# Pooled v of the first batch summed on TensorE out of loaded v tiles, and the first FFN conversion queued behind the 13th attention unit

## The chip, the cores and the metric

The kernel runs on one core of one Trainium2 chip. The metric is the device time of one execution in microseconds (us), and the time of a kernel is the median of its runs. Of the engines, PE is TensorE (PEld its weight loads), DVE is VectorE, ACT is ScalarE, POOL is GpSimd, and SP only issues DMA transfers. Each engine takes its instructions strictly in the order in which they stand in its queue.

## What is computed

Attention runs over 2 batches, 8 heads, 576 positions and 64 values per head, in two forms whose outputs are added. Then comes a softplus FFN (1152 tokens, 512 to 2048 to 512), and then eight gated experts. Cut to what matters here:

```python
q_d = q.reshape(B, H, Sd, factor, D).mean(axis=3)      # factor 4, Sd = 144
k_d = k.reshape(B, H, Sd, factor, D).mean(axis=3)
v_d = v.reshape(B, H, Sd, factor, D).mean(axis=3)
out_up = np.repeat(sm_attn(q_d, k_d, v_d), factor, axis=2)
mask = np.abs(pos[:, None] - pos[None, :]) < factor
...
attn_out = out_up + out_local                          # local: softmax inside the mask
h = x @ w_in                                           # x: attn_out as 1152 x 512
x = (np.maximum(h, 0.0) + np.log1p(np.exp(-np.abs(h)))) @ w_out
...
out += P[:, e:e + 1] * (np.maximum(x @ w1[e], 0.0) @ w2[e])   # eight experts
```

## The kernel before

**Attention** is a list of units, each with four steps. A `pooled` unit (batch, half of the 144 pooled queries, pair of heads) makes scores `pd` from pooled q and k, exponentials `e`, transposes `ptd`, and the product `pvd` with the pooled v, `vd`. A `local` unit (batch, tile of 116 queries, half of the heads) makes masked scores `pl`, exponentials, transposes `ptl`, the product `pvl` with the loaded v tile `vw` (122 positions by 8 heads by 64 values and a one), and the transposed sum `xf`, which POOL splits into a high and a low part of `x`, the input of the FFN (a CAST and a subtraction). `emit` runs the units staggered, two units apart from step to step. There are 8 pooled and 10 local units in each batch, and unit number 9, 13 and so on below is the place in this mixed list, counted from 0. `warm` adds matmuls of zeros, `pz`, which keep TensorE busy while the first loads are under way.

**Pooling.** `pool_qk` sums q over groups of four positions on DVE (`qd`) and k on POOL (`ks`, `kd`), and ACT scales k. `load_vd` loads v a second time in another layout (`vr`, 640 KB for each half of the positions), and adds the four positions in two steps, `vs` and `vd`: on DVE for the first batch, on POOL for the second. Four `vr` tiles pass through two buffers of the pool `raw`, which the FFN weights use after them.

**FFN weights** arrive as doubles in tiles `raw` (1 MB each). `prep(n)` turns one tile into a high and a low part `w`: ACT makes `cs`, `cm` and the high part, DVE six operations in between (`cm` twice, `ch`, `ca`, `ch`, `cs`), POOL (DVE later) the low part. Products `ph` of the first FFN layer need `w` and `x`; `py` is the second layer.

**Order.** The table `at` says ahead of which unit an extra step is written: the loads of batch 1 at unit 1, `load_vd(1)` and the first two `raw` at 9, `pool_qk(1, p)` at 11 to 14, `prep(0)` to `prep(3)` at 16, 19, 23 and 29, the first FFN products from 22 on. A scheduler then sets the order on each engine within the bounds of the data and of `issue_after`, which keeps what is written inside it behind a named instruction. `local` step 3 loads the `vw` tile that is needed three tiles later, since there are three buffers.

Of the kernel before, what the change touches and what calls it, by code (L numbers as in the profile page):

```python
# [21 lines left out]
P = 128  # L22
# [54 lines left out]
class Net:  # L77
# [128 lines left out]
    def attention_pools(self, stack):  # L206
        tc = self.tc
        self.convp = stack.enter_context(tc.tile_pool(name="conv", bufs=1, side="right"))
        self.qkp = stack.enter_context(tc.tile_pool(name="qkp", bufs=NPAIR, side="right"))
        self.vwp = stack.enter_context(tc.tile_pool(name="vwp", bufs=3, side="right"))  # L210
# [35 lines left out]
    def pool_qk(self, b, p):  # L246

        nc = self.nc
        qd = self.atp.tile([P, 2, G], F32, tag="qd", name=f"qd{b}{p}", bufs=NPAIR)
        nc.vector.tensor_reduce(  # L250
            out=qd, in_=self.qT[b, p].rearrange("p h (g f) -> p h g f", f=POOLF), op=ALU.add, axis=AX.X
        )
        s = self.atp.tile([P, G, 2], F32, tag="ks", name=f"ks{b}{p}", bufs=2)
        k = self.kT[b, p]
        v = k.rearrange("p (g f) -> p g f", f=POOLF)
        nc.gpsimd.tensor_tensor(s, v[:, :, 0:2], v[:, :, 2:4], ALU.add)
        kd = self.atp.tile([P, G], F32, tag="kd", name=f"kd{b}{p}", bufs=NPAIR)
        nc.gpsimd.tensor_tensor(kd, s[:, :, 0], s[:, :, 1], ALU.add)
# [9 lines left out]
    def load_vd(self, b):  # L268
        nc = self.nc
        vd = self.atp.tile([GH, 2, H, DA], F32, tag="vd", name=f"vd{b}", bufs=2)  # L270
        nc.gpsimd.memset(vd[:, :, :, D:DA], 1.0)
        for hf in range(2):
            r = self.rawp.tile([GP, POOLF, DM], F32, tag="raw", name=f"vr{b}{hf}")
            nc.sync.dma_start(out=r, in_=self.a["vp"][b, hf].rearrange("p (f d) -> p f d", f=POOLF))
            s = self.convp.tile([GH, 2, DM], F32, tag=("ch", "cs")[hf], name=f"vs{b}{hf}", bufs=1)
            e = nc.vector if b == 0 else nc.gpsimd
            e.tensor_tensor(s, r[:GH, 0:2], r[:GH, 2:4], ALU.add)
            sv = s.rearrange("p f (h d) -> p f h d", h=H)
            e.tensor_tensor(vd[:, hf, :, 0:D], sv[:, 0], sv[:, 1], ALU.add)
        self.vd[b] = vd  # L280
        self.upT[b] = self.atp.tile([P, NPAIR, G], F32, tag="upT", name=f"upT{b}", bufs=2)

    def softmax_exp(self, ps, n, m, k, tag):

        nc = self.nc
        nm = self.atp.tile([m, n], F32, tag="nm" + tag, name="nm")
        nc.vector.tensor_reduce(out=nm, in_=ps, op=ALU.max, axis=AX.X, negate=True)
        e = self.atp.tile([m, n, k], F32, tag="e" + tag, name="e", bufs=3 if tag == "l" else 2)
        for j in range(n):
            nc.scalar.activation(e[:, j], ps[:, j], AF.Exp, bias=nm[:, j : j + 1])  # L290
        return e

    def pooled(self, b, hf, p):
# [25 lines left out]
            st["pt"] = pt  # L319

        def s3():
            ps = self.psa.tile([P, 512], F32, tag="a", name="pvd")[:GH, : 2 * DA].rearrange("p (j d) -> p j d", j=2)
            for j in range(2):
                for kh in range(2):
# [22 lines left out]
    def local(self, b, t, g):  # L347
# [33 lines left out]
        def s3():  # L381
            ps = self.psa.tile([P, 512], F32, tag="a", name="pvl")[:nq, : 4 * DA].rearrange("p (j d) -> p j d", j=4)
            for j in range(4):
                nc.tensor.matmul(  # L384
                    ps[:, j], lhsT=st["pt"][:, j], rhs=self.vw[b, t][:KW, 4 * g + j], start=True, stop=True
                )
            if g == 1 and NQT * b + t + 3 < B * NQT:
                self.load_vw(*divmod(NQT * b + t + 3, NQT))
# [326 lines left out]
    def run(self):  # L715
# [18 lines left out]
            self.pool_qk(0, p)  # L734
        self.constants()
        self.load_vd(0)
        for t in range(3):
            self.load_vw(0, t)

        def emit(items, rest):  # L740
# [25 lines left out]
                self.load_qk(1, p)  # L766

        def load_rest():
            self.load_vd(1)
            self.load_raw(1)  # L770

        def prep(n, lag):
# [4 lines left out]
                self.prep(n)  # L777


        at = {1: [load_second], 9: [load_rest]}  # L780
        for p in range(NPAIR):
            at.setdefault(11 + p, []).append(lambda p=p: self.pool_qk(1, p))
        for n, lag, u in zip(range(2 * NFT), (1, 1, 0, 0), (16, 19, 23, 29)):
            at.setdefault(u, []).append(lambda n=n, lag=lag: prep(n, lag))
        one, two, after = self.l1(0, 0, 1), self.l2(0, 0, 1), self.l1(0, 1, 1)
        for m, u in zip(one + two[:2], (22, 24, 26, 28, 30, 32)):
# [154 lines left out]
def arrange(i):  # L941
# [17 lines left out]
    m = [np.where(np.abs(r + o - c) < POOLF, f(0), f(-1e9)) for o in OFF]  # L959
    m = np.concatenate([np.stack(m, 1), np.zeros((P - QT, len(OFF), KW), f)], 0)  # L960
    out["mask"] = np.ascontiguousarray(m.astype(f))
    out["wg"] = np.ascontiguousarray(i["moe2_w_gate"].reshape(KD, P, E).transpose(1, 0, 2))

    def up(w):
# [36 lines left out]
```

## Time and profile before

| what | value |
|---|---|
| median of 3 runs (lowest to highest) | 1067.16 us (1064.26 to 1067.43) |
| the profiled execution | 1065.39 us, of which its span 1063.6 us |
| PE busy, share of the span | 1042.9 us, 98% |
| DVE, ACT, POOL busy | 74%, 41%, 16% |
| mean granted TensorE clock | 0.997 |

The span runs from the first instruction to the last, and 1.8 us of the execution lie outside it. A busy share is an average over the whole span. The attention, where the change is made, takes the first tenth of it; after that PE is busy all the time.

### The profile page before, as it was taken

The page shows a single profiled execution, that of the slowest core. Times are in us where ns is not written, and L with a number is a line of the kernel's source. Part 1 is how long each engine was busy: PE and PEld are TensorE (multiplying, and loading weights), DVE is VectorE, ACT ScalarE, POOL GpSimd, SP SyncE. Part 2 cuts the span into 40 slices and gives each one's busy share as a digit, 9 for nine tenths or more (in the row PEclk, how much of TensorE's full clock was granted, in tenths as well). Part 3 has the DMA queues.
Part 4 walks back from the last instruction along what each step waited for, and adds up shares of the span by engine and source line. Part 5 has one row for each costly group of instructions (what it writes and reads, how often), then busy time and mean ns, then how long its engine had stood idle before and what let it go on. Part 6 is the DMA issues. An engine that isn't in the chain of part 4 may idle for free.

```text
span 1063.6 us, 16117 instructions
## 1 busy us (share of the span) xinstructions
PE 1042.9 (98%) x6421; PEld 959.9 (90%) x6421; DVE 783.1 (74%) x1466; ACT 435.4 (41%) x815; POOL 165.8 (16%) x218
## 2 busy tenths in 40 slices
PE   7899999999999999999999999999999999999998
PEld 4789999999998899898989989898998989899896
DVE  6698699999997687784947658484765848576572
ACT  4688687766743433241413324141331414133130
POOL 3463300001112220211202011120201112020000
PEclk9899999999999999999999999999999999999999
DMA  9541032222111221111211111121111112110003
GB/s 250 163 153 62 2 120 79 79 80 80 41 40 40 79 80 40 40 41 39 80 40 40 41 40 41 40 80 40 40 40 40 41 40 79 40 41 1 1 2 89
DMA packets 13035, 63.99 MB, mean 60 GB/s; under 512 B 1760, under 2 KB 2016, under 8 KB 6496
## 3 DMA queue, kind: packets, MB, share of 16 engines
q1 hardware_dynamic: 12320, 61.79, 17.8%
q10 hardware_dynamic: 640, 1.18, 0.4%
q8 instruction: 50, 0.82, 0.3%
q14 instruction: 25, 0.20, 0.1%
HBM read 60.60 MB, written 2.36 MB: 59 GB/s over the span
## 4 chain that ended last, share of the span: by engine, by line
PE 87%; DVE 8%; ACT 2%; DMA 2%; POOL 1%; issue 1%; SPq 0%; DVEq 0%; ACTq 0%
PE po L586 37%; PE pu L537 33%; PE ph L444 7%; PE py L486 6%; PE pl L364 1%; DVE h L465 1%; DMA vr<-in_vp 1%; PE pvl L384 1%; DMA k<-in_k 1%; DVE r L461 1%; DVE l L462 1%; PE pvd L325 1%; DVE l L463 1%; DVE yp L498 0%; PE ptl L376 0%
## 5 line engine op out<-in xcount | busy, mean ns | idle before, releaser
L537 PE MATMUL pu<-T,a 128*128 128x320 f32 (+1 forms) x2688 | 354.2, 293 | 1.4 <-DVE yp L498 1.4
L537 PEld LDWEIGHTS pu<-T,a 128*128 128x128 f32 x2688 | 351.4, 188 | 3.0 <-issue 1.6
L608 DVE SCALAR_TENSOR_TENSOR acc<-po,prob,acc 128x512 f32<-128x512 f32 x126 | 94.1, 749 | 173.5 <-PE po L586 173.5
L586 PE MATMUL po<-w,h 128*128 128x512 f32 x960 | 221.3, 390 | 0.0
L586 PEld LDWEIGHTS po<-w,h 128*128 128x128 f32 x960 | 179.9, 188 | 37.3
L188 ACT CAST w<-raw 128x1024 fp32r<-128x1024 f32 x32 | 33.4, 1052 | 271.4 <-PE po L586 271.4
L586 PE MATMUL po<-w,h0a 128*128 128x512 f32 x576 | 142.3, 390 | 0.6 <-DVE w L189 0.6
L157 POOL TENSOR_TENSOR s<-raw 128x256 f32<-128x256 f32 x32 | 28.5, 891 | 677.6 <-DVE a L168 473.0
L586 PEld LDWEIGHTS po<-w,h0a 128*128 128x128 f32 x576 | 107.3, 188 | 22.5 <-DVE w L189 1.0
L486 PE MATMUL py<-h,w 128*128 128x384 f32 x576 | 104.0, 336 | 1.3 <-DVE h L465 0.8
L444 PE MATMUL ph<-x,w 128*128 128x384 f32 x576 | 104.1, 336 | 0.0
L486 PEld LDWEIGHTS py<-h,w 128*128 128x128 f32 x576 | 99.7, 188 | 2.3 <-DVE h L465 1.3
L444 PEld LDWEIGHTS ph<-x,w 128*128 128x128 f32 x576 | 99.8, 188 | 0.0
L549 ACT ACTIVATE h<-c 128x320 fp32r<-128x320 f32 x128 | 58.6, 468 | 79.8 <-DVE c L560 79.8
L550 DVE SCALAR_TENSOR_TENSOR h<-c,h 128x320 fp32r<-128x320 f32 x128 | 68.1, 540 | 0.3
L560 DVE TENSOR_TENSOR c<-v,pu 128x256 f32<-128x256 f32 (+1 forms) x128 | 57.8, 451 | 11.1 <-PE pu L537 8.2
L549 ACT ACTIVATE h0a<-c 128x256 fp32r<-128x256 f32 x96 | 37.5, 417 | 50.7 <-DVE c L560 50.4
L189 DVE TENSOR_TENSOR w<-raw,w 128x1024 fp32r<-128x1024 f32 x32 | 39.0, 1220 | 22.1 <-ACT w L188 22.1
L586 PE MATMUL po<-w,h0b 128*128 128x512 f32 x192 | 54.2, 389 | 0.0
L586 PEld LDWEIGHTS po<-w,h0b 128*128 128x128 f32 x192 | 36.0, 188 | 7.5
L558 ACT COPY p<-pu 128x256 f32<-128x256 f32 (+1 forms) x64 | 25.1, 392 | 36.1 <-PE pu L537 34.5
L550 DVE SCALAR_TENSOR_TENSOR h0a<-c,h0a 128x256 fp32r<-128x256 f32 x96 | 39.1, 420 | 0.8 <-ACT h0a L549 0.3
(141 smaller groups left out, 1243.2 us busy)
## 6 DMA issues: line engine op xcount, KB each, us to landing
raw<-in_w SPq DMA_DIRECT2D x48, 1024.0 KB, 4.9
vw<-in_vw SPq DMA_DIRECT2D x10, 260.0 KB, 2.9
vr<-in_vp SPq DMA_DIRECT2D x4, 640.0 KB, 8.8
k<-in_k SPq DMA_DIRECT2D x8, 288.0 KB, 6.2
out<-acc SPq DMA_DIRECT2D x5, 256.0 KB, 2.0
q<-in_q SPq DMA_DIRECT2D x8, 144.0 KB, 5.9
out<-acc SPq DMA_DIRECT2D x8, 128.0 KB, 2.3
q0a<-in_q ACTq DMA_DIRECT2D x4, 144.0 KB, 5.6
```

The source lines that it names most:

```text
L157: nc.gpsimd.tensor_tensor(s[:, 0], a21, a22, ALU.add)
L188: nc.scalar.copy(w[:, 0], raw)
L189: nc.vector.tensor_tensor(w[:, 1], raw, split(w[:, 0]), ALU.subtract)
L444: nc.tensor.matmul(ps[:, i], lhsT=wv[:, a, k, fo : fo + P], rhs=x[:, b, k], start=(n == 0), stop=(n == 3 * KD - 1),)
L486: nc.tensor.matmul(ps[:, a], lhsT=w[:, i, d * P : (d + 1) * P], rhs=h[:, j, f], start=(n == 0), stop=(n == 3 * NFT - 1),)
L537: nc.tensor.matmul(ps, lhsT=w[:, x, a, k], rhs=t[:, y, b, k], start=(m == 0), stop=(m == 5))
L549: act = nc.scalar.activation(hi, src, AF.Relu)
L550: dve = nc.vector.scalar_tensor_tensor(lo, src, 0.0, split(hi), ALU.max, ALU.subtract)
L558: nc.scalar.copy(to, ps)
L560: nc.vector.tensor_tensor(to, src, ps, ALU.add)
L586: nc.tensor.matmul(ps, lhsT=self.h[s, i, f][:, at * P : (at + 1) * P], rhs=w[:, j], start=(n == 0), stop=(n == 3 * NFT - 1),)
L608: nc.vector.scalar_tensor_tensor(acc, ps, pe, acc, ALU.mult, ALU.add)
```

## The change

The first batch no longer loads `vr`. A small matrix of zeros and ones, `pool` (128 x 288), is loaded, and `sum_vw` multiplies the five loaded `vw` tiles by its columns: three matmuls of 512 columns in fp32 for each half of the positions, added up in PSUM (`pvs`), and one ACT copy for each half into `vd`. `vw` gets five buffers, all five loads of batch 0 stand at the start, and those of batch 1 are written tile by tile as the old ones are used up. The second batch keeps its way, but its `load_vd` and the first `raw` loads are written at unit 13 and behind the last `kd` sum of `pool_qk`; `pool_qk(1, p)` moves from units 11 to 14 to units 9 to 12, each behind the exponentials that are the last written at that point; `prep(0)` moves from unit 16 to unit 13 and goes behind the maximum and the exponentials of the unit just begun.

```diff
         for hf in range(2):
             r = self.rawp.tile([GP, POOLF, DM], F32, tag="raw", name=f"vr{b}{hf}")
...
-            e = nc.vector if b == 0 else nc.gpsimd
-            e.tensor_tensor(s, r[:GH, 0:2], r[:GH, 2:4], ALU.add)
+            nc.gpsimd.tensor_tensor(s, r[:GH, 0:2], r[:GH, 2:4], ALU.add)
...
+    def sum_vw(self):
+        nc = self.nc
+        for hf in range(2):
+            ps = self.psa.tile([P, 512], F32, tag="a", name="pvs")[:GH]
+            parts = [(t, at) for t, h, at in POOLS if h == hf]
+            for n, (t, at) in enumerate(parts):
+                nc.tensor.matmul(
+                    ps,
+                    lhsT=self.pool[:KW, at : at + GH],
+                    rhs=self.vw[0, t][:KW, :, 0:D],
+                    start=(n == 0),
+                    stop=(n == len(parts) - 1),
+                )
+            nc.scalar.copy(self.vd[0][:, hf, :, 0:D], ps.rearrange("p (h d) -> p h d", h=H))
...
         def s3():
+            if (b, hf, p) == (0, 0, 0):
+                self.sum_vw()
...
-        for t in range(3):
+        for t in range(NQT):
             self.load_vw(0, t)
...
         def load_rest():
-            self.load_vd(1)
+            with self.tc.issue_after(self.pooled_k.ins):
+                self.load_vd(1)
             self.load_raw(1)
...
+        def pool_second(p):
+            with self.tc.issue_after(self.exp.ins):
+                self.pool_qk(1, p)
+
+        def prep_first():
+            with self.tc.issue_after(self.top.ins), self.tc.issue_after(self.exp.ins):
+                self.prep(0)

-        at = {1: [load_second], 9: [load_rest]}
+        at = {1: [load_second], 13: [load_rest, prep_first]}
         for p in range(NPAIR):
-            at.setdefault(11 + p, []).append(lambda p=p: self.pool_qk(1, p))
-        for n, lag, u in zip(range(2 * NFT), (1, 1, 0, 0), (16, 19, 23, 29)):
+            at.setdefault(9 + p, []).append(lambda p=p: pool_second(p))
+        for n, lag, u in zip(range(1, 2 * NFT), (1, 0, 0), (19, 23, 29)):
```

What TensorE's queue holds where the first pooled products begin, before the change (`vd_179` is the pooled v of batch 0; `kd` and `qd` with numbers are the pooled k and q of one pair of heads):

```order
L316 MATMUL ptd<-ident,e 72x72 x2
L325 MATMUL pvd<-vd_179,ptds 72x65 x4
L301 MATMUL pd<-kd_133,qd_129 72x144
L301 MATMUL pd<-kd_141,qd_137 72x144
L316 MATMUL ptd<-ident,e 72x72 x4
L325 MATMUL pvd<-vd_179,ptds 72x65 x4
```

And at the same place with the change (`vw_184` to `vw_192` are the five v tiles):

```order
L355 MATMUL ptd<-ident,e 72x72 x2
L313 MATMUL pvs<-vw_184,pool 72x512
L313 MATMUL pvs<-vw_186,pool 72x512
L313 MATMUL pvs<-vw_188,pool 72x512 x2
L313 MATMUL pvs<-vw_190,pool 72x512
L313 MATMUL pvs<-vw_192,pool 72x512
L224 LDWEIGHTS z
L224 MATMUL pz<-z 128x512
```

Six matmuls of 512 columns and two pairs of warm-up matmuls stand between the transposes `ptd` and the first product with `vd_179`; ahead of that `ptd`, a row not shown, the last scores of the first four units (`pd<-kd_165,qd_161`) have moved in front of the warm-up matmuls. An fp32 matmul that is one row here appears as two instructions in the trace.

ACT's queue where the first FFN conversion begins, before (`raw_480` is the first weight tile; `e<-pl` are exponentials of a local unit, `e<-pd` of a pooled one):

```order
L318 COPY ptds<-ptd 72x288
L343 COPY upT_191<-pxd 128x72
L126 ACTIVATE cm<-raw_480 128x1024
L124 ACTIVATE cs<-raw_480 128x1024
L290 ACTIVATE e<-pd,nm 72x144 x2
L259 ACTIVATE kd_649<-kd_649 128x144
L378 COPY ptls<-ptl 122x464
L259 ACTIVATE kd_693<-kd_693 128x144
L290 ACTIVATE e<-pl,nm 116x122 x4
```

And with the change, from the same exponentials `e<-pd` on (`raw_663` is now the first weight tile):

```order
L329 ACTIVATE e<-pd,nm 72x144 x2
L279 ACTIVATE kd_606<-kd_606 128x144
L280 ACTIVATE k_206<-k_206 128x576
L419 COPY ptls<-ptl 122x464
L329 ACTIVATE e<-pl,nm 116x122 x4
L357 COPY ptds<-ptd 72x288
L384 COPY upT_181<-pxd 128x72
L329 ACTIVATE e<-pl,nm 116x122 x4
L419 COPY ptls<-ptl 122x464
L329 ACTIVATE e<-pl,nm 116x122 x4
L146 ACTIVATE cm<-raw_663 128x1024
```

The first conversion step stood ahead of the fifth local unit's exponentials and of a pooled unit's; it now stands behind the seventh local unit's.

POOL's queue where it sums the second batch's v, before:

```order
L256 TENSOR_TENSOR ks_691<-k_210 128x288
L277 TENSOR_TENSOR vs_471<-vr_469 72x1024
L277 TENSOR_TENSOR vs_476<-vr_474 72x1024
L279 TENSOR_TENSOR vd_467<-vs_471 72x8x64
L279 TENSOR_TENSOR vd_467<-vs_476 72x8x64
L258 TENSOR_TENSOR kd_649<-ks_647 128x144
L419 CAST x_553<-xf 128x2x116
```

And with the change:

```order
L276 TENSOR_TENSOR ks_604<-k_206 128x288
L278 TENSOR_TENSOR kd_567<-ks_565 128x144
L460 CAST x_558<-xf 128x2x116
L278 TENSOR_TENSOR kd_606<-ks_604 128x144
L291 MEMSET vd_650 72x16
L302 TENSOR_TENSOR vs_655<-vr_653 72x1024
L302 TENSOR_TENSOR vs_660<-vr_658 72x1024
L461 TENSOR_TENSOR x_558<-xf,x_558 128x2x116
L304 TENSOR_TENSOR vd_650<-vs_655 72x8x64
```

The sums of v have moved behind the last two sums of k and the first cast of x.

## Rows read from the trace of the kernel before

**Rows 1.** Page, part 2: TensorE's granted clock in 40 slices, tenths.

```profile
PEclk9899999999999999999999999999999999999999
```

**Rows 2.** Windows: length, busy us of PE, PEld, DVE, ACT, POOL, clock, DMA.

```profile
45.00:50.00 5.00, 5.00 (x31) 4.88 (x31) 2.79 (x5) 2.83 (x11) 0.00 (x0) 0.50 0.00 0
...
50.00:90.00 40.00, 37.74 (x348) 36.29 (x347) 36.17 (x93) 34.02 (x89) 22.57 (x25) 1.00 0.34 114
90.00:100.00 10.00, 9.80 (x84) 9.37 (x82) 10.00 (x24) 7.89 (x23) 5.36 (x3) 1.00 0.39 133
```

**Rows 3.** Chain that ended last, first 100 us: start, us, what.

```profile
24.18 0.51 PE pvd L325 x8
24.69 0.50 PE pd L301 x4
...
26.08 0.21 PE pl L356
...
36.07 0.49 PE pd L301 x4
...
37.60 0.83 PE pl L364 x8
...
44.95 1.63 PE pl L364 x8
...
50.69 0.77 PE pvl L384 x8
```

**Rows 4.** Timeline of DVE, 14 to 22 us: start, us, what, idle before.

```profile
14.86 1.22 DVE L277 TENSOR_TENSOR vs<-vr 72x1024 f32<-72x1024 f32 x1 [0.78 <-DMA vr<-in_vp]
...
18.73 1.22 DVE L277 TENSOR_TENSOR vs<-vr 72x1024 f32<-72x1024 f32 x1 [1.93 <-DMA vr<-in_vp]
19.88 1.34 DVE L250 TENSOR_REDUCE qd<-q0b 128x288 f32<-128x1152 f32 x1
```

**Rows 5.** Timeline of the first conversion, 36 to 50 us, all engines.

```profile
36.16 2.66 SPq L108 DMA_DIRECT2D raw<-in_w  x2
...
41.64 1.13 ACT L126 ACTIVATE cm<-raw 128x1024 f32<-128x1024 f32 x1 [3.99 <-DMA raw<-in_w]
...
42.81 0.70 DVE L127 TENSOR_SCALAR cm<-cm 128x1024 f32<-128x1024 f32 x1 [1.59 <-ACT cm L126]
...
44.39 0.56 PE L356 MATMUL pl<-mask,identb 116*116 116x488 bf16 x1 [3.77 <-ACT e L290]
...
47.20 0.68 DVE L129 TENSOR_SCALAR cm<-cm 128x1024 int32<-128x1024 int32 x1
...
48.20 1.21 DVE L130 SCALAR_TENSOR_TENSOR ch<-raw,cm 128x1024 int32<-128x1024 int32 x1
```

**Rows 6.** Loads of q0b and vw: issues (duration ns, first and last start), landing.

```profile
L244 ACTq DMA_DIRECT2D q0b<-in_q x4: 472/472/517, 4.6 to 9.5; - x4
...
DMA to landing us min/median/max: 5.1/6.2/7.3
...
L265 SPq DMA_DIRECT2D vw<-in_vw x10: 327/328/683, 10.1 to 96.9; - x10
...
DMA to landing us min/median/max: 2.5/2.9/9.2
```

**Rows 7.** Prices: warm-up matmuls in the timeline, ACT's copy out of PSUM by form.

```profile
11.62 1.89 PE L204 MATMUL pz<-z 128*128 128x512 bf16 x8
...
L378 ACT COPY ptls<-ptl 122x464 f32<-122x464 f32 x16 | 8.8, 547 | 5.2 <-PE ptl L376 5.2
```

**Rows 8.** Timeline of POOL, 33 to 66 us.

```profile
33.79 4.67 POOL L277 TENSOR_TENSOR vs<-vr 72x1024 f32<-72x1024 f32 x2 [3.21 <-DVE rrd L335]
...
41.24 0.37 POOL L419 CAST x<-xf 128x232 fp32r<-128x232 f32 x1
...
62.02 3.34 POOL L419 CAST x<-xf 128x232 fp32r<-128x232 f32 x1 [1.75 <-DVE xf L406]
```

More of the change, by code (lines that the diff above doesn't have):

```diff
@@ L43, with pooling @@
 OFF = sorted({QT * t - WIN[t] for t in range(NQT)})
+SHIFT = [QT * t - WIN[t] for t in range(NQT)]
+SPANS = [(t, hf) for t in range(NQT) for hf in range(2) if QT * t < (hf + 1) * POOLF * GH and QT * (t + 1) > hf * POOLF * GH]
+def pooling():
+    at, cols, n = [], [], 0
+    for o in OFF:
+        spans = [(t, hf) for t, hf in SPANS if SHIFT[t] == o]
+        first = [GH * hf - QT // POOLF * t for t, hf in spans]
+        lo, hi = min(first), max(first) + GH
+        at += [(t, hf, n + f - lo) for (t, hf), f in zip(spans, first)]
+        cols += [(o, g) for g in range(lo, hi)]
+        n += hi - lo
+    return at, cols
+POOLS, POOL_COLS = pooling()
+PW = len(POOL_COLS)
 NRING = 6
@@ L209, in attention_pools @@
         self.qkp = stack.enter_context(tc.tile_pool(name="qkp", bufs=NPAIR, side="right"))
-        self.vwp = stack.enter_context(tc.tile_pool(name="vwp", bufs=3, side="right"))
+        self.vwp = stack.enter_context(tc.tile_pool(name="vwp", bufs=NQT, side="right"))
         self.atp = stack.enter_context(tc.tile_pool(name="atp", bufs=3, side="right"))
@@ L257, in pool_qk @@
         kd = self.atp.tile([P, G], F32, tag="kd", name=f"kd{b}{p}", bufs=NPAIR)
-        nc.gpsimd.tensor_tensor(kd, s[:, :, 0], s[:, :, 1], ALU.add)
+        self.pooled_k = nc.gpsimd.tensor_tensor(kd, s[:, :, 0], s[:, :, 1], ALU.add)
         nc.scalar.activation(kd, kd, AF.Copy, scale=SCALE / (POOLF * POOLF))
@@ L271, in load_vd @@
         nc.gpsimd.memset(vd[:, :, :, D:DA], 1.0)
+        self.vd[b] = vd
+        self.upT[b] = self.atp.tile([P, NPAIR, G], F32, tag="upT", name=f"upT{b}", bufs=2)
+        if b == 0:
+            self.pool = self.convp.tile([P, PW], F32, tag="cs", name="pool", bufs=1)
+            nc.sync.dma_start(out=self.pool, in_=self.a["pool"])
+            return
         for hf in range(2):
@@ L275, in load_vd @@
             s = self.convp.tile([GH, 2, DM], F32, tag=("ch", "cs")[hf], name=f"vs{b}{hf}", bufs=1)
-            e = nc.vector if b == 0 else nc.gpsimd
-            e.tensor_tensor(s, r[:GH, 0:2], r[:GH, 2:4], ALU.add)
+            nc.gpsimd.tensor_tensor(s, r[:GH, 0:2], r[:GH, 2:4], ALU.add)
             sv = s.rearrange("p f (h d) -> p f h d", h=H)
-            e.tensor_tensor(vd[:, hf, :, 0:D], sv[:, 0], sv[:, 1], ALU.add)
-        self.vd[b] = vd
-        self.upT[b] = self.atp.tile([P, NPAIR, G], F32, tag="upT", name=f"upT{b}", bufs=2)
+            nc.gpsimd.tensor_tensor(vd[:, hf, :, 0:D], sv[:, 0], sv[:, 1], ALU.add)
+    def sum_vw(self):
[12 more added lines that the diff above has]
+            nc.scalar.copy(self.vd[0][:, hf, :, 0:D], ps.rearrange("p (h d) -> p h d", h=H))
     def softmax_exp(self, ps, n, m, k, tag):
@@ L286, in softmax_exp @@
         nm = self.atp.tile([m, n], F32, tag="nm" + tag, name="nm")
-        nc.vector.tensor_reduce(out=nm, in_=ps, op=ALU.max, axis=AX.X, negate=True)
+        self.top = nc.vector.tensor_reduce(out=nm, in_=ps, op=ALU.max, axis=AX.X, negate=True)
         e = self.atp.tile([m, n, k], F32, tag="e" + tag, name="e", bufs=3 if tag == "l" else 2)
         for j in range(n):
-            nc.scalar.activation(e[:, j], ps[:, j], AF.Exp, bias=nm[:, j : j + 1])
+            self.exp = nc.scalar.activation(e[:, j], ps[:, j], AF.Exp, bias=nm[:, j : j + 1])
         return e
@@ L386, in s3 @@
                 )
-            if g == 1 and NQT * b + t + 3 < B * NQT:
-                self.load_vw(*divmod(NQT * b + t + 3, NQT))
+            if g == 1 and b + 1 < B:
+                self.load_vw(b + 1, t)
             rs = self.atp.tile([nq, 4, 1], F32, tag="rsl", name="rsl")
@@ L961, in arrange @@
     out["mask"] = np.ascontiguousarray(m.astype(f))
+    w = np.zeros((P, PW), f)
+    for j, (o, g) in enumerate(POOL_COLS):
+        nq = max(min(QT, S - QT * t) for t in range(NQT) if SHIFT[t] == o)
+        for r in range(POOLF * g + o, POOLF * g + o + POOLF):
+            if o <= r < o + nq:
+                w[r, j] = 1
+    out["pool"] = w
     out["wg"] = np.ascontiguousarray(i["moe2_w_gate"].reshape(KD, P, E).transpose(1, 0, 2))
```

## The prediction

> **What bounds the kernel now.** I read the page first. TensorE is busy 98% of the span, and its clock is at nine tenths or more in every slice but the second, where it shows 8 [rows 1], so nothing can be won except where TensorE idles or runs slowly, and that is near the start. The windows by stage show where: from 45 to 50 us the granted clock is 0.50, the 1.2 GHz level of the two [rows 2]. The chain of waits shows what comes before: TensorE's local scores take 0.83 us at 37.60 and 1.63 us, the double, at 44.95; they are back at the usual speed by 50.69 [rows 3]. The timeline gives the cause: at 44.39 TensorE ends a wait of 3.77 us for ACT's exponentials, and ACT had sat 3.99 us, until 41.64, in front of `cm` of the first FFN conversion, whose 1 MB weight tile had not landed [rows 5]. All exponentials behind it in ACT's queue waited too. The tile was late because it was issued only at 36.16 [rows 5], into a buffer that POOL was still emptying: the `vs` sums of the second batch began at 33.79 and take 4.67 us for two [rows 8]. So this episode costs 3.8 us of idling, and the stretch from 44.4 to 50.4, 6.0 us long at half speed, another 3.0.
>
> After 50 us two engines are near their limit at once. TensorE is busy 37.74 of 40 us and then 9.80 of 10, DVE 36.17 of 40 and then 10.00 of 10 [rows 2].
>
> At the very start DVE stands for 0.78 and 1.93 us in front of `vs`, waiting for the two loads of `vr`, and the sum `qd` of the last q half is queued behind the second one, at 19.88 [rows 4]. The first product with pooled v then starts at 24.18, and the second local unit's scores at 26.08 [rows 3].
>
> **The change, step by step.** *DVE's sums go.* Two `vs` of 1.22 us [rows 4] and their two `vd` leave DVE. They lie in the time before 24 us, so they count only through what they hold up.
>
> *The sums on TensorE.* `qd` of the last q half needs only its data. The last q0b issue is at 9.5 and lands after 5.1 to 7.3 us, median 6.2 [rows 6], so at 15.7; `qd` takes 1.34 [rows 4], to 17.0. Then come two scores `pd` of half the 0.50 us that four pieces take [rows 3], a pair of transposes of 0.1, and nine warm-up matmuls, of 1.89/8 = 0.24 us each [rows 7], 2.1 together: the sums start at 17.0 + 0.25 + 0.1 + 2.1 = 19.5. No row shows an fp32 matmul of 512 columns. The nearest are the `pd` pieces, 0.125 us for 144 columns [rows 3]; each fp32 matmul is two pieces, so 512/144 × 0.125 = 0.44 us for a piece and 12 × 0.44 = 5.3 us for six matmuls. From below the bound is six warm-up matmuls of the same 512 columns in bf16, 1.4 us; from above 10.6 us, if the clock were at its lower level. I take 5.3, since type and engine are those of `pd`. The sums end at 24.8. Their last tile is the fifth `vw`, whose issue I put near 12.3, behind two more than before (the first was at 10.1); even with the longest landing, 9.2 us [rows 6], it is there at 21.5, ahead of its matmul at 23.9. The copy of the first half by ACT (about 0.55, as the copy of similar width [rows 7]) is hidden by the second half's matmuls, and that of the second half by the four warm-up matmuls, the transposes and scores that now stand there; without these it would add 0.6. From 24.8: two warm-up matmuls 0.5 and a transpose pair 0.1 to 25.4, then what took 26.08 - 24.18 = 1.9 before, less one transpose pair, and two more warm-up matmuls, 2.2 together. The second local unit starts at 27.6 instead of 26.08: **1.5 us lost**. With the bounds of the matmuls this term runs from 2.4 us won to 6.8 lost.
>
> *The stall.* From 26 to 40.6 us TensorE works almost without a gap, so it reaches the place of the stall at 42.1. POOL starts `vs` behind the last `kd`, which waits for the scores that ended at 36.07 + 0.49 = 36.6 before [rows 3] and end at 38.1 now, so it begins at about 38.6; half of 4.67 later, at 41.0, the first buffer is free and the weight tile is issued. It took 41.64 - 36.16 = 5.5 us before [rows 5], so it lands at 46.5. The new place of `cm` is behind the seventh local unit's exponentials, which I put at 47.0 from TensorE's order at full speed. The tile is 0.5 us early: it is later than before, but what asks for it is later still. No other load is slowed on this account: the loads of batch 1's `vr` and `vw` stand ahead of the tile on SP and wait for work that is done by 38. **3.8 us and 3.0 us won.** The clock goes with the wait: before the 3.77 us of idling it was full, behind it it was half for 6 us, and full again once TensorE had worked through that [rows 2, 3]. The Trainium skill, in "TensorE: Matmul & The Clock Gate", section "What's actually happening", says that the throttled clock is the default and activity releases it. By that rule the 3.0 belong to the idling and go with it, and the trace agrees; were the slow stretch due to something else, the sum below would lack these 3.0.
>
> TensorE alone would thus gain 3.8 + 3.0 - 1.5 = 5.3 us by the time that was 50 us.
>
> *The conversion moves into full time.* Before, three DVE operations of the first conversion (0.70, 0.68 and 1.21 [rows 5], 2.6 together) lay in the stall, and DVE had nothing better to do. Now they start after 47.0. The stretch that was 50 to 100 us begins at 44.7 and holds DVE's old 36.17 + 10.00 = 46.2 us [rows 2] and these 2.6: 48.8. DVE's share was 36.17/40 = 0.90 where it shared the bound with TensorE, and 1.00 in the last 10 us. Now it is behind TensorE for longer, so I take 0.96, between the two: 50.8 us, and 1.0 more because the conversion can't begin at 44.7 but only once ACT has made `cm`. It ends at 44.7 + 50.8 + 1.0 = 96.5 instead of 100: **1.8 of the 5.3 us are given back**. The order pulls FFN products forward on TensorE, ahead of attention steps, which keeps TensorE from idling all of that time, but doesn't add DVE time. The ends: at share 1.00 the gain is 5.5, more than TensorE allows, so 5.3; at 0.90 it is 0.1.
>
> **Sum.** -3.8 - 3.0 + 1.5 + 1.8 = -3.5 us. From the profiled execution, 1065.4, that is 1061.9. This execution lies 1.8 us below the median of the three runs, 1067.2, from which it would be 1063.7. I take the middle, 1062.8.
>
> **Rivals.** *TensorE keeps all.* DVE's work finds room because FFN products now stand between the attention steps, and the early start of q and k of batch 1 costs nothing. For it: DVE reached 10.00 of 10 [rows 2]. Against it: 0.90 in the 40 us before. Gain 5.3 and, if the sums on TensorE are nearer to their lower bound, up to 8: 1058 to 1061.
>
> *The wait moves on to POOL.* The third and fourth `x` casts now fall into the first conversion on DVE instead of into an empty stretch. Such a cast took 0.37 us at 41.24 and 3.34 at 62.02, in the middle of the second conversion [rows 8], and `xf` has two buffers, so DVE stops when POOL is late. Two casts at 3.34 instead of 0.8 cost 5.1 us; if 3.5 of them reach DVE's path, the gain is gone: about 1066. For it: the one long cast of before. Against it: other casts near the conversions took under a microsecond. The Trainium skill says in "SBUF — State Buffer", section "SBUF: two separate sides", that VectorE and GpSimd share a pair of ports, which a VectorE operation with two SBUF inputs or a GpSimd operation holds for its whole length. By that rule each cast can wait out one whole DVE operation after another; the row at 62.02 bears it out for one cast.
>
> *The change doesn't remove the wait.* If POOL comes to `vs` 4 us later than I put it, the weight tile lands at 50.5 and ACT stands in front of `cm` for 3.5 us as before; the sums' 1.5 us come on top of no gain: 1066 to 1068.
>
> *Slower.* DVE can't hold 0.90 in the full stretch, since more of its conversions now meet POOL's work. The point is 48.8/(100 - 44.7 - 1.0) = 0.90: below it the change loses. At 0.85 the stretch takes 57.4 us and ends at 103.1, 3.1 us later than before: 1070. For it: 0.90 was DVE's share with TensorE at the same load [rows 2].
>
> **Chances and range.** Forecast (a gain of 2 to 5) 0.55, all kept 0.15, POOL 0.12, wait not removed 0.06, slower 0.12. About 0.3%, 3.2 us, is what a measurement of this kernel can tell from no change. Of the forecast's 0.55, two thirds lie above that: faster 0.36 + 0.15 = 0.51. Same: the other 0.19 and the two rivals that come out near zero, 0.37. Slower 0.12. The range leaves out the upper half of "slower" and the far end of "all kept": 1059.0 to 1068.0; the forecast's own is 1060.5 to 1065.
>
> **What would show it.** In the profile of the changed kernel: twelve pieces `pvs` of about 0.44 us from about 19.5 to 24.8; the second local unit's scores at about 27.6; no wait of ACT over 1 us in front of `cm`, at about 47; the clock at 1.00 from 40 to 50; DVE at 0.95 or more from 47 to 97; TensorE's chain unbroken from about 97 on. The prediction is wrong if the weight tile lands behind the exponentials, if a wait for `xf` or POOL takes over after 47 us, or if the sums are held up by a late `vw`.

## The result, and the profile after

The changed kernel takes 1073.51 us (median of 6 runs, 1071.23 to 1076.56), the kernel before on the same chip 1065.87 (6 runs, 1063.85 to 1067.43). The ratio is 1.0072, with a 95% interval of 1.0054 to 1.0090: **7.6 us slower**, where 1062.8 and a range of 1059.0 to 1068.0 were predicted. The profiled execution took 1071.23 us, its span 1069.4, which is 5.8 more than the span before. It is the fastest of the six, 2.3 us under their median, so the profile accounts for 5.8 of the 7.6 us.

First the places where the prediction looked for its gain. TensorE and ACT in the timeline of the changed kernel (start, duration, engine, what; idle time ahead of it and what ended that, in brackets), and then one row of the kernel before:

```profile
18.93 5.32 PE L313 MATMUL pvs<-vw,pool 122*72 122x512 f32 x12
...
26.84 0.37 PE L397 MATMUL pl<-mask,identb 116*116 116x488 bf16 x1
...
46.11 1.19 ACT L146 ACTIVATE cm<-raw 128x1024 f32<-128x1024 f32 x1
...
60.48 0.37 PE L397 MATMUL pl<-mask,identb 116*116 116x488 bf16 x1
```

```profile
65.83 0.37 PE L356 MATMUL pl<-mask,identb 116*116 116x488 bf16 x1
```

The twelve pieces of the sums take 5.32 us, as forecast, and the second local unit starts at 26.84 in this view, 0.9 later than the 25.91 that the same view has for before. `cm` stands at 46.11 with no idle time ahead of it: the wait of 3.99 us [rows 5] is gone, and with it TensorE's 3.77 us and the slow clock behind them. At 60.48 the 11th local unit's scores begin. Before, this was at 65.83. TensorE is 5.3 us ahead here, which is what the prediction gave it.

The start itself can't be read to a microsecond from one profile. In the ten profiled kernels of this document that have the sums, TensorE's matmuls up to the second local unit stand in the same order, and yet this unit starts anywhere between 26.84 us (the changed kernel) and 29.57 (e6); in the six without the sums, between 25.91 (before) and 29.89 (e14). The 0.9 us is smaller than this scatter. Counted from the second local unit on, the 11th follows after 39.92 us before and after 33.64 with the change, 6.3 us sooner, and in the nine other kernels below that have the new order and the second conversion in its place after 33.6 to 33.8. That gain is firm.

Then the windows, where the answer to [rows 2] stands (length; busy us of PE, PEld, DVE, ACT, POOL; granted clock; DMA):

```profile
40.00:50.00 10.00, 9.78 (x100) 9.56 (x100) 8.64 (x25) 9.31 (x28) 8.25 (x9) 1.00 0.63 238
50.00:60.00 10.00, 8.04 (x74) 7.34 (x72) 10.00 (x23) 8.37 (x21) 7.47 (x5) 1.00 0.47 158
60.00:70.00 10.00, 6.77 (x46) 5.49 (x45) 6.80 (x18) 5.17 (x13) 9.43 (x11) 0.84 0.31 107
70.00:80.00 10.00, 9.26 (x80) 8.85 (x79) 6.38 (x17) 6.64 (x16) 2.52 (x3) 0.99 0.09 27
80.00:90.00 10.00, 8.23 (x72) 7.79 (x71) 10.00 (x25) 8.33 (x24) 6.49 (x4) 1.00 0.32 107
90.00:100.00 10.00, 8.04 (x67) 7.33 (x66) 9.91 (x20) 8.16 (x22) 4.78 (x3) 0.88 0.31 106
100.00:110.00 10.00, 10.00 (x64) 9.70 (x63) 5.89 (x16) 3.17 (x10) 3.15 (x7) 0.78 0.01 2
```

DVE, full at 10.00 from 50 to 60, is busy only 6.80 and 6.38 of ten between 60 and 80. TensorE is not full either, and its clock falls twice, in 60 to 70 and in 90 to 110. When the two engines that share the bound both stand idle, they wait for each other or for a third. The timeline names it:

```profile
62.92 3.84 POOL L460 CAST x<-xf 128x72 fp32r<-128x72 f32 x2
...
63.19 0.67 DVE L153 TENSOR_SCALAR ca<-raw 128x1024 int32<-128x1024 int32 x1
...
63.92 0.67 DVE L155 TENSOR_SCALAR ch<-ch 128x1024 int32<-128x1024 int32 x1
...
65.19 1.21 DVE L154 SCALAR_TENSOR_TENSOR cs<-ca,cs 128x1024 f32<-128x1024 int32 x1
...
66.56 0.47 PE L485 MATMUL ph<-x,w 128*128 128x384 f32 x1 [2.84 <-POOL x L460]
...
68.00 0.39 ACT L357 COPY ptds<-ptd 72x288 f32<-72x288 f32 x1 [3.58 <-PE ptd L355]
...
70.79 3.38 PE L485 MATMUL ph<-x,w 128*128 128x384 f32 x18
71.02 0.16 DVE L431 TENSOR_SCALAR rsl<-pvl 112x4 f32<-112x4 f32 x1 [4.21 <-PE pvl L425]
...
74.46 0.39 DVE L447 TENSOR_TENSOR xf<-pxl,upT 128x224 f32<-128x224 f32 x1 [2.55 <-PE pxl L441]
```

Read it from the middle. The first FFN product `ph` waits 2.84 us for POOL's cast of the last 36 tokens of `x` that it needs. The row at 62.92 holds two casts, of 36 and of 80 tokens. Narrower windows of the timeline show the cast of 36 tokens alone, the needed one and the next of the same shape:

```profile
62.92 3.58 POOL L460 CAST x<-xf 128x72 fp32r<-128x72 f32 x1
...
67.49 0.24 POOL L460 CAST x<-xf 128x72 fp32r<-128x72 f32 x1
```

The long one lies beside `ca`, `ch` and `cs` of the second FFN conversion on DVE and ends at 66.50, just behind `cs` (66.40). Behind `ph` in TensorE's queue stand `ptd` and `pvl`, which have all that they need, and, behind 18 more pieces of `ph`, `pxl`, which needs what DVE makes of `pvl`. So ACT waits 3.58 us for `ptd`, DVE 4.21 us for `pvl` and 2.55 for `pxl`. And the clock follows, in windows of 2 us:

```profile
64.00:66.00 2.00, 0.00 (x0) 0.00 (x0) 2.00 (x4) 0.42 (x2) 2.00 (x1) 1.00 0.58 123
66.00:68.00 2.00, 1.44 (x7) 1.10 (x8) 0.80 (x3) 0.00 (x1) 2.00 (x7) 0.71 0.95 401
68.00:70.00 2.00, 2.00 (x7) 1.58 (x7) 0.00 (x0) 1.98 (x4) 2.00 (x3) 0.50 0.03 8
```

TensorE does nothing from 64 to 66, and then works at 0.50, the 1.2 GHz level: the old stall with a new cause, some 20 us later.

### The profile page after: what moved, and what is told of

It reads as the page before. It is cut to its first block, busy times and chain, and to the rows that moved or that the text cites. A ratio compares the mean times of both kernels' runs of the same rounds, so it can differ in the third digit from the quotient of the medians.

```text
span 1069.4 us, 16124 instructions
## 1 busy us (share of the span) xinstructions
PE 1049.7 (98%) x6433; PEld 962.3 (90%) x6433; DVE 783.6 (73%) x1462; ACT 436.6 (41%) x817; POOL 170.9 (16%) x218
## 4 chain that ended last, share of the span: by engine, by line
PE 84%; DVE 6%; ACT 1%; issue 0%; DVEq 0%
PE po L627 37%; PE pu L578 32%; PE ph L485 6%; PE py L527 6%; DVE h L506 1%; DVE r L502 1%; DVE l L503 1%; DVE yp L539 0%; PE pvl L425 0%; DVE l L504 0%; PE pl L405 0%; DVE T L568 0%; DVE cs L154 0%; DVE a L188 0%; DVE ch L150 0%
```

## Where TensorE's time goes, in all kernels

A sum over windows of 2 us makes the profiled executions comparable from 30 us on: the time in which TensorE ran no matmul, plus its busy time multiplied by (1 - granted clock). For before, 42 to 60 us gives 2.5 idle + 3.0 slow = 5.5. "DVE idle" is the time without DVE work from 60 to 80. All in us; the last columns are the ratio to the kernel before on the same chip.

| kernel | 30-42 | 42-60 | 60-80 | 80-96 | 96-110 | DVE idle | ratio (95%) |
|---|---|---|---|---|---|---|---|
| before | 2.0 | 5.5 | 1.8 | 0.3 | 0.7 | 1.7 | 1 |
| after | 0.4 | 2.0 | 5.5 | 2.0 | 4.6 | 6.8 | 1.0072 (1.0054-1.0090) |
| e1 sums only | 6.0 | 1.8 | 1.7 | 0.5 | 1.4 | 1.1 | 1.0057 (1.0044-1.0069) |
| e2 order only | 0.7 | 1.6 | 6.5 | 2.0 | 5.4 | 7.8 | 1.0074 (1.0061-1.0087) |
| e3 product held behind | 0.4 | 1.7 | 5.8 | 0.6 | 1.5 | 3.7 | 1.0036 (1.0022-1.0049) |
| e4 cast on ACT | 0.2 | 1.1 | 6.2 | 1.8 | 5.5 | 6.2 | 1.0072 (1.0058-1.0085) |
| e5 second conversion late | 0.2 | 1.1 | 0.5 | 2.2 | 5.6 | 2.1 | 1.0035 (1.0022-1.0048) |
| e6 x past POOL | 0.2 | 1.1 | 2.8 | 0.5 | 0.7 | 0.5 | 0.9994 (0.9983-1.0005) |
| e7 held behind + past POOL | 0.3 | 1.0 | 5.2 | 2.0 | 5.7 | 0.3 | 1.0087 (1.0072-1.0101) |
| e8 order only + held behind | 0.2 | 1.3 | 5.0 | 0.7 | 0.9 | 3.5 | 1.0010 (0.9998-1.0022) |
| e9 first piece as in e6, through POOL | 0.4 | 1.8 | 5.3 | 2.0 | 4.5 | 6.3 | 1.0044 (1.0030-1.0058) |
| e10 before + past POOL | 0.1 | 6.7 | 1.3 | 3.2 | 1.9 | 1.5 | 1.0038 (1.0025-1.0052) |
| e11 order only + past POOL | 0.2 | 1.1 | 2.8 | 0.5 | 0.7 | 0.5 | 0.9976 (0.9967-0.9984) |
| e12 second late + past POOL | 0.4 | 0.9 | 0.7 | 0.8 | 0.7 | 1.8 | 0.9959 (0.9947-0.9971) |
| e13 second layer held | 0.3 | 1.6 | 6.1 | 1.7 | 5.5 | 6.8 | 1.0083 (1.0069-1.0096) |
| e14 = e12 without sums | 0.2 | 1.1 | 0.7 | 0.6 | 0.9 | 2.3 | 0.9960 (0.9946-0.9974) |

Before against after: 5.1 won by 60 us, 9.3 lost behind it, 4.2 in all; with the 0.9 of the start in these two executions that is 5.1 of the span's 5.8.

## The experiments

**Theory A**: the loss comes from where the first FFN products stand in TensorE's queue. **B**: DVE has too much to do after 50 us, wherever the pieces stand. **C**: the sums on TensorE cost it. The first four kernels made a **theory D** of A: what the products wait for, POOL's work on `x` beside DVE's conversion, is the cause.

**e1, the sums alone** (the order table of before):

```diff
-        at = {1: [load_second], 13: [load_rest, prep_first]}
+        at = {1: [load_second], 9: [load_rest]}
...
-            at.setdefault(9 + p, []).append(lambda p=p: pool_second(p))
-        for n, lag, u in zip(range(1, 2 * NFT), (1, 0, 0), (19, 23, 29)):
+            at.setdefault(11 + p, []).append(lambda p=p: self.pool_qk(1, p))
+        for n, lag, u in zip(range(2 * NFT), (1, 1, 0, 0), (16, 19, 23, 29)):
```

> The sums on TensorE and the five v buffers alone; the order table is that of before, so the first conversion stands ahead of the exponentials again and the first FFN products stand behind two more attention steps. Theory A (the loss comes from the first FFN products standing too early in TensorE's queue): the wait of 3.8 us and the slow stretch of before are back, the products wait no more than before, the sums cost 0.9 us at the start: 1065.9 + 0.9, 1065 to 1068. Theory B (the conversion comes too late and DVE can't catch up): the same 1065 to 1068. Theory C (the sums on TensorE are what costs): the loss of 7.6 us stays, 1072 to 1075.

1070.15 us, ratio 1.0057: a miss for all three. On its chip the kernel before takes 1063.82, so e1 lies 6.1 us above it, far from the 0.9 of A and B and not far below the 7.6 of C. The timeline of e1 shows a stall that none foresaw:

```profile
37.67 1.13 ACT L144 ACTIVATE cs<-raw 128x1024 f32<-128x1024 uint32 x1 [4.38 <-POOL vd L304]
...
40.19 0.57 PE L397 MATMUL pl<-mask,identb 116*116 116x488 bf16 x1 [4.52 <-ACT upT L384]
```

The first conversion's `cs` shares its buffer with POOL's `vs` of the second batch, and the scheduler put `cs` and `cm` ahead of the copies that TensorE needs. The stretch from 30 to 42 us loses 6.0 instead of 2.0, and 42 to 60 loses 1.8 instead of 5.5: together 7.8 against 7.5, so the stall of before has moved rather than grown. It doesn't explain the 6.1 us, and most of them stay open. This kernel alone doesn't give the price of the sums and doesn't rule out C; the pairs below do.

**e2, the order alone** (the new table and its waits, with DVE's `vs` and three `vw` buffers as before).

> The new order table alone; DVE sums the first batch's v as before. TensorE's first FFN products stand as early as in the changed kernel. Theory A: the wait of the first product for the cast of x is 2 to 4 us again, DVE idles about 7 us between 65 and 80 us, and the time is the changed kernel's less the 0.9 us of the sums: 1070 to 1074. Theory B: the same. Theory C: the stall is won and nothing lost, 1059 to 1064.

1071.91, ratio 1.0074. C falls: without the sums the whole loss is there, with DVE idle for 7.8 us between 60 and 80.

**e3, the first product held** behind the transposes of the ninth local unit:

```diff
...
+        def turned(m):
+            with self.tc.issue_after(self.turned.ins):
+                m()
...
-        for m, u in zip(one + two[:2], (22, 24, 26, 28, 30, 32)):
-            at.setdefault(u, []).append(m)
+        for n, (m, u) in enumerate(zip(one + two[:2], (23, 24, 26, 28, 30, 32))):
+            at.setdefault(u, []).append((lambda m=m: turned(m)) if n < 1 else m)
```

> The changed kernel, with the first FFN product held behind the transposes of the ninth local unit, where it stood before; conversion, sums and loads stay as in the changed kernel. Theory A: the attention steps no longer stand behind a product that waits, DVE's idle time between 65 and 80 us falls from 7 to under 2, and 5 to 8 us come back: 1065 to 1069. Theory B: the conversion is as late as in the changed kernel, so at most 1 or 2 us come back: 1071 to 1074.

1067.47, ratio 1.0036: about half comes back, which speaks for A, but not all. In its timeline the long cast is still there (`self.turned` is the last `pxl` written):

```profile
63.85 3.85 POOL L460 CAST x<-xf 128x72 fp32r<-128x72 f32 x2
...
68.11 4.19 PE L485 MATMUL ph<-x,w 128*128 128x384 f32 x12
...
73.34 1.18 ACT L144 ACTIVATE cs<-raw 128x1024 f32<-128x1024 uint32 x1 [4.83 <-POOL w L157]
```

The attention steps no longer wait for it, but POOL comes late to the low part `w`, and ACT waits 4.83 us for that. The twelve pieces of `ph` take 4.19 us, mostly at the lower clock; twelve at full clock, in e7's timeline, take 2.33.

**e4, the cast of the fourth tile on ACT**, the subtraction still on POOL:

```diff
+                if (b, t) == (0, 3):
+                    nc.scalar.copy(hi, xf[:, :, n : n + m])
+                else:
+                    nc.gpsimd.tensor_copy(hi, xf[:, :, n : n + m])
-                nc.gpsimd.tensor_copy(hi, xf[:, :, n : n + m])
```

> The changed kernel, with the casts of x of the first batch's fourth tile made by ACT's copy instead of POOL; TensorE's queue stays as it is. Theory A with the cast as its cause (the product waits because POOL's cast of 3.84 us lies across DVE's conversion): the wait of 2.84 us in front of the first product falls below 1 and 2 to 5 us come back: 1068 to 1072. If the product would have to wait anyway, for the steps that precede the cast: 1072 to 1075.

1072.21, ratio 1.0072: nothing won. TensorE's queue did change, against the expectation: the first product now stands behind the transposes `ptd`. It goes on time, but the next pieces need the low part of `x`, and in its timeline POOL's subtraction is now the long one:

```profile
65.29 4.28 POOL L464 TENSOR_TENSOR x<-xf,x 128x72 fp32r<-128x72 f32 x4 [0.61 <-ACT x L461]
65.48 0.42 PE L488 MATMUL ph<-x,w 128*128 128x384 f32 x1
...
68.36 1.41 PE L488 MATMUL ph<-x,w 128*128 128x384 f32 x5 [2.23 <-POOL x L464]
```

So it isn't the cast: whichever POOL operation comes at this place is stretched. That is theory D.

**e5, the second conversion late** (its DVE work taken away from beside the casts):

```diff
-        for n, lag, u in zip(range(1, 2 * NFT), (1, 0, 0), (19, 23, 29)):
+        for n, lag, u in zip(range(1, 2 * NFT), (0, 0, 0), (22, 25, 29)):
```

> The changed kernel, with the second FFN conversion written behind the last sum of the first batch's fourth tile instead of two steps earlier (and the third two units later), so that its DVE operations no longer lie beside the casts of x that the first product needs; the first conversion stays where the change put it. The first product then also stands behind the transposes ptd. Theory D (POOL's operations on x are stretched while DVE runs a conversion, and TensorE waits for them): the casts that took 3.84 us take under 1.2, the wait in front of the first product falls from 2.84 to under 0.5, and 5 us or more come back: 0 to 3 us above the kernel before. Theory B (DVE has too much to do in this stretch, wherever the pieces stand): the second conversion only ends later, and the time stays 5 to 8 us above the kernel before.

1068.38, ratio 1.0035, between the two. At the disputed place its timeline shows D right:

```profile
61.79 0.50 POOL L460 CAST x<-xf 128x72 fp32r<-128x72 f32 x2 [0.28 <-DVE xf L447]
...
63.34 1.94 POOL L460 CAST x<-xf 128x72 fp32r<-128x72 f32 x2 [0.27 <-DVE rrd L376]
```

The needed casts take 0.50 us, the first product waits for nothing, and 60 to 80 loses 0.5 us instead of 5.5. But 96 to 110 still loses 5.6. One wait of that stretch is plain in e5's timeline:

```profile
96.50 2.62 POOL L157 TENSOR_TENSOR w<-cs,ch 128x1024 fp32r<-128x1024 f32 x1 [2.33 <-DVE cs L154]
...
96.95 2.58 DVE L506 TENSOR_TENSOR h<-l,h 128x384 fp32r<-128x384 f32 x1
...
99.59 0.69 PE L527 MATMUL py<-h,w 128*128 128x384 f32 x1 [2.11 <-DVE h L506]
```

Here POOL's work is in DVE's way: `h`, which takes 0.53 us at 89.11, takes 2.58 beside POOL's low part of `w`, and `py` waits 2.11 us for it. Another `h` takes 2.55 at 82.72, again beside that operation.

**e6, the first 36 tokens of the fourth tile past POOL**, cast on ACT and subtraction on DVE:

```diff
+                if (b, t, c) == (0, 3, 0):
+                    nc.scalar.copy(hi, xf[:, :, n : n + m])
+                    nc.vector.tensor_tensor(lo, xf[:, :, n : n + m], split(hi), ALU.subtract)
+                else:
...
```

> The changed kernel, with cast and subtraction of the first 36 tokens of the fourth tile on ACT and DVE, so that POOL has no part in what the first product waits for. The first product stands as early on TensorE as in the changed kernel (ahead of pvl and pxl). Theory D: the wait of 2.84 us falls below 1, and 3 to 6 us come back: 1 to 4 us above the kernel before. Theory A (standing early is bad whatever the product waits for): DVE's subtraction comes behind its other work, the wait stays at 2 us or more, and the time 5 us or more above before.

1064.45 (12 runs), ratio 0.9994: the whole loss is back, more than any theory gave it. Its timeline:

```profile
65.64 1.93 POOL L464 CAST x<-xf 128x160 fp32r<-128x160 f32 x1
...
65.98 0.25 ACT L461 CAST x<-xf 128x72 fp32r<-128x72 f32 x1
...
66.50 0.42 PE L489 MATMUL ph<-x,w 128*128 128x384 f32 x1
...
67.55 0.22 DVE L462 TENSOR_TENSOR x<-xf,x 128x72 fp32r<-128x72 f32 x1
...
68.13 2.50 PE L489 MATMUL ph<-x,w 128*128 128x384 f32 x13
```

Fourteen pieces of `ph` run ahead of `pxl` and wait for nothing; cast and subtraction take 0.25 and 0.22 us. POOL's cast of the other tokens is stretched to 1.93 as ever, and nobody waits for it. The clock stays at 1.00 from 40 to 130. Standing early is not what is bad: A, as first put, falls. One thing had moved as well: the product stood behind `ptd` here. e9 tests that.

**e7, the edits of e3 and e6 together.**

> Both together: the first product held behind the ninth local unit's transposes, and the first 36 tokens of the fourth tile past POOL. Theory D: POOL's low part of the second conversion is no longer late behind its work on x (ACT waited 4.83 us and DVE 2.74 us for it with the product held behind alone), the slow stretch from 66 to 74 us shrinks, and the time is 0 to 2 us above the kernel before. Theory B: as with the product held behind alone, 3 to 4 us above.

1073.71, ratio 1.0087, the slowest of all and a plain miss. TensorE loses in three stretches (5.2, 2.0, 5.7 us), though DVE idles only 0.3 us between 60 and 80. At 104.81 `py` waits 3.10 us for POOL's low part of `w`. The scheduler had set the third conversion's DVE steps as one block ahead of attention's. Two edits that help alone don't add up; what exactly makes the first 5.2 us here is not settled.

**e8, e2 with e3's edit.**

> The new order table with the first product held behind, but DVE sums the first batch's v as before (no sums on TensorE, three v buffers). If the sums cost what the start of the changed kernel shows, 0.9 us, it is 0 to 2 us faster than the changed kernel with the product held behind, so 2 to 4 us above the kernel before. If the sums are what is left of the loss, it is at the time of the kernel before or up to 3 us faster than it.

1066.14, ratio 1.0010, against 1.0036 with the sums: 2.8 us in this pair, between the two expectations. They needn't be the sums' price: from 60 to 80 us e3's profile has 3.0 us of slow clock and e8's none, though the longest wait of TensorE there is 1.41 us in both.

**e9, the first product behind `ptd` alone, where e6 had it, and POOL's work as in the changed kernel** (e3's edit, with another instruction for `self.turned`):

```diff
-                    nc.tensor.transpose(ps[:, j, kh], st["e"][:, j, kh * GH : (kh + 1) * GH], ident[:GH, :GH])
+                    self.turned = nc.tensor.transpose(ps[:, j, kh], st["e"][:, j, kh * GH : (kh + 1) * GH], ident[:GH, :GH])
```

> The changed kernel with the first product held behind the transposes ptd alone, which is where it stood with the 36 tokens past POOL; it still stands ahead of pvl and pxl, and cast and subtraction of x stay on POOL. Theory D (POOL's work on x): the wait for x is still 2 us or more and the loss stays, 5 to 8 us above the kernel before. If the place behind ptd was what brought the time back, 0 to 2 us above before.

1071.16, ratio 1.0044 (1.0030 to 1.0058): 4.7 us above the kernel before, at the edge of D's range, 5.3 above e6 by the ratios and 3 below the changed kernel. In its timeline:

```profile
63.73 3.84 POOL L460 CAST x<-xf 128x72 fp32r<-128x72 f32 x2
...
67.37 0.69 PE L485 MATMUL ph<-x,w 128*128 128x384 f32 x1 [2.59 <-POOL x L460]
```

The wait of 2.59 us and the idle DVE are back, so the wait comes from POOL's part, and the place behind `ptd` alone doesn't remove it; in e4 the first product stood there too, and nothing was won. But only the first piece stands where e6 had it. Of the pieces behind it, 11 run ahead of `pvl` here and none in e6, and up to `pxl` 24 pieces run in all, against 14. What of the 5.3 us is the wait and what these pieces isn't separated.

**e10, the kernel before with e6's edit.**

> The kernel before with the first 36 tokens of the fourth tile past POOL and nothing else. There the first conversion lay in the stall and POOL's casts of those tokens took 0.50 us, with no wait of the first product for POOL. Theory D: nothing to win, within 2 us of the kernel before. If past POOL is simply the better way everywhere, it is 3 us or more faster than before.

1070.31, ratio 1.0038: 4 us slower. Neither reading expected that. The scheduler pulled the first products forward here too, and ACT still waited for the weight tile (4.20 us): the stall stretch loses 6.7, and 80 to 110 another 5.1, against 5.5 and 1.0 before. The profile is no clean witness, though: it is of the slowest of seven runs, and 3.5 of the 6.4 us by which its span is longer lie ahead of the second local unit (29.40 against 25.91), where the matmuls stand in the same order as before. Past POOL is no better in itself; it paid where the product's wait for POOL was long.

**e11, e2 with e6's edit, and e12, the edits of e5 and e6 together.**

> The new order table and the 36 tokens past POOL, with DVE's sums of v as before (no sums on TensorE). By the start of the changed kernel the sums cost 0.9 us, and by the pair with the product held behind 2.4 us: 0 to 3 us faster than with sums and past POOL, so 1 to 4 us faster than the kernel before.

> The second conversion late and the 36 tokens past POOL, both on the changed kernel. If the late second conversion loses at 90 to 105 us because the third and fourth conversion then crowd DVE, the time stays at 2 to 5 us above the kernel before, with a clock of 0.5 near 102 us, though the first products come as early as with either. If POOL's work on x was still what held it up, 0 to 2 us faster than before.

e11: 1063.50, ratio 0.9976, 1.9 us better than with the sums. Against e2, which differs by the 36 tokens alone, it is 10.4 us faster: without the sums, too, taking POOL out of the product's way brings back the whole loss. e12: 1061.70, ratio 0.9959, 4.4 us faster than before and more than either reading gave. The second and third conversions are as late as in e5, and the second slow stretch is gone, so their lateness alone doesn't make it. TensorE loses under 1 us in each stretch from 60 on, and its windows have:

```profile
60.00:70.00 10.00, 10.00 (x91) 9.66 (x90) 9.85 (x25) 7.43 (x23) 5.58 (x9) 1.00 0.32 86
```

**e13, the first second-layer products `py` held** one unit later in the changed kernel, behind `pvl` (`self.turned` is set by it):

```diff
...
+        for n, (m, u) in enumerate(zip(one + two[:2], (22, 24, 26, 28, 33, 34))):
+            at.setdefault(u, []).append((lambda m=m: turned(m)) if n >= 4 else m)
```

> The changed kernel with the first two products of the second FFN layer (py) held behind the product pvl that stood behind them, one unit later; the first products of the first layer stay where they are. In the changed kernel py stood ahead of pxd and pl, waited 0.75 us for h, and the clock was 0.50 from 98 to 104 us. If the place of py makes the second slow stretch, the 4.6 us of idle and slow TensorE time between 95 and 110 us fall below 2 and 2 to 4 us come back: 3 to 5 us above the kernel before. If the second stretch only passes on what DVE and ACT lost in the first one, it stays, a little later: 5 to 8 us above before.

1073.41, ratio 1.0083: nothing won, 96 to 110 loses 5.5. The place of `py` doesn't make the second slow stretch. What lies on the path there is shown by the chain that ended last, in the changed kernel (start, us, what):

```profile
91.24 0.46 DVE h L506
91.70 0.60 DVE cm L149
92.31 0.09 issue
92.40 1.53 DVE ch L150
...
96.76 1.13 DVE cs L154
...
98.64 0.47 DVE l L504
99.16 2.29 PE py L527 x6
```

From 91 to 99 the path is DVE alone, with a conversion and the softplus mixed; TensorE then starts `py` at the lower clock. DVE had stood idle 6.8 us at 60 to 80, and is full from 80 to 98.

**e14, e12 without the sums on TensorE** (the new table, DVE's `vs`).

> The new order table, the second conversion late and the 36 tokens past POOL, with DVE's sums of v as before (no sums on TensorE). Against the same with the sums on TensorE, which was 4.1 us faster than the kernel before, it tells the price of the sums: by the pairs so far 1 to 3 us faster still, 5 to 7 us faster than before. If the sums then lie in idle time anyway, equal, 4 us faster than before.

1060.32, ratio 0.9960, the same as e12. With nothing else waiting the sums cost nothing that can be measured. Over the four pairs (changed kernel/e2, e3/e8, e6/e11, e12/e14) the difference is -0.2, 2.8, 1.9 and 0 us, each uncertain by about 2; in e6/e11 the table's rows are equal, so what differs there lies outside 30 to 110 us. The mean is 1.1, about as uncertain as it is large.

## Why the prediction was wrong

*The start*, +1.5 us: the sums take 5.32 us, as worked out, but that they delay the second local unit by 1.5 us is not shown. The 0.9 between the two profiles is less than the scatter of the start from execution to execution, 2.7 us with the sums and 4.0 without. Over the four pairs the sums cost 1.1 us on average, uncertain by about 1, which fits 1.5 as it fits 0.9.

*The stall*, -3.8 and -3.0: right. From the second to the 11th local unit TensorE gains 6.3 of these 6.8 us, and 42 to 60 loses 2.0 instead of 5.5. That it is 5.3 us ahead there, the prediction's own 3.8 + 3.0 - 1.5, is in part luck, since both terms came out smaller in these two profiles.

*The give-back*, +1.8: here it failed. The sentence is "The order pulls FFN products forward on TensorE, ahead of attention steps, which keeps TensorE from idling all of that time, but doesn't add DVE time." It read the new order as overlap, at no cost, and never asked when the pulled product's input is ready. It needs POOL's cast, the cast lies beside the second conversion, and everything that feeds DVE stood behind the product. So TensorE lost 5.5 us idling and running slowly from 60 to 80, instead of 1.8, DVE stood idle for 6.8 instead of 1.7, and the share that the prediction took as 0.96 came out as 43.41/51, in the windows of the changed kernel:

```profile
45.00:96.00 51.00, 43.08 (x366) 39.85 (x365) 43.41 (x100) 39.06 (x98) 31.91 (x29) 0.97 0.30 104
```

That is 0.85, the share of the rival "slower", which gave 1070 and had a chance of 0.12; but the share fell because DVE stood idle behind TensorE, where that rival has POOL's work slow it. That was there too (`cm` took 2.19 us at 56.39), but a slowed operation counts as busy, and e6 has the same row without the loss. The give-back was not 1.8 but 5.3 + 5.8 = 11 us of the span. One of the prediction's own signs of being wrong, that a wait for POOL takes over after 47 us, is what came.

*The rivals.* "The wait moves on to POOL" had the mechanism (a cast of 3.34 us [rows 8]) and the wrong place: it looked for the harm in DVE's wait for the two `xf` buffers and priced it at 3.5. The harm is in TensorE's wait for `x`, with ACT's and DVE's input queued behind it, and a second loss at the lower clock on top. The rule it cited from the Trainium skill, "SBUF — State Buffer", section "SBUF: two separate sides" (VectorE and GpSimd lock a shared port pair against each other for a whole instruction), fits the direction, and e4 to e6 agree: beside the conversion the cast (3.58 us), the subtraction (four in 4.28) and the cast of the other tokens (1.93) are all long, and without it the pair of casts takes 0.50. That POOL is held by a port is not shown by any run. By "one whole DVE operation after another" the 3.58 us would be `ca`, `ch` and `cs`, 2.55 us, and what lies between them; the trace can't tell whether those in between hold POOL as well.

*The second slow stretch* was in no part of the prediction. It goes with DVE's idle time at 60 to 80 in most kernels: at 6 us or more (after, e2, e4, e9, e13) 96 to 110 loses 4.5 to 5.5, at 4 or less 0.7 to 1.9. e5 and e7 are exceptions, with 2.1 and 0.3 us of idle DVE and 5.6 and 5.7 lost. So handing on is the likely reading for the changed kernel, not a proven one. In e5 two DVE operations were stretched beside POOL's `w`, and `py` waited for the second; whether that makes its whole stretch was not tested, and e7's is open.

## What to carry to other kernels

Where a new order puts an instruction ahead of others on an in-order engine, look up when its latest input is made, on every engine that makes it; what stands behind it pays for the wait, and here it paid more than the stall that was removed. Before moving DVE work into a new stretch, look at which POOL operations lie there and who waits for them; the few small ones that are on the path can go to another engine. A gain at one place of a chain of several full engines is worth what reaches the end: follow it there, unit by unit, before adding it up.

## What the runs showed of the hardware

POOL's small operations stretch by more than one DVE operation: a cast of 128x72 took 0.24 us at 67.49, and the one at 62.92 took 3.58 while DVE ran eight operations back to back, of which the longest was 1.21. It goes the other way too: `cm` on DVE, 0.68 us at 74.77 in the changed kernel, took 2.59 beside POOL's `w` of 2.37 in e7's timeline:

```profile
70.50 2.37 POOL L157 TENSOR_TENSOR w<-cs,ch 128x1024 fp32r<-128x1024 f32 x1
70.83 2.59 DVE L147 TENSOR_SCALAR cm<-cm 128x1024 f32<-128x1024 f32 x1
```

A single wait of TensorE of about 3 us or more (2.84 here, 3.77 before [rows 5], 4.52 in e1) was followed each time by a stretch at a clock of 0.50, which cost 1.5, 3.0 and 2.1 us more; that part of the price is easily left out of a sum. But the clock also fell where the longest single wait was shorter, 1.41 us in e3 and 0.99 in the changed kernel just ahead of 98 us, and it stayed at 1.00 in e8, with a longest wait of 1.41 and 5.0 us of idling in all from 60 to 80. So these runs don't tell how short a wait is safe.
